# Sparse attention and a gated convolution block on one core: the first head pair turned in float32, mask rows spread by copies, half of the last convolution moved to VectorE, a new written order

## The chip, the cores and the metric

The kernel runs on one core of a Trainium2 chip. The metric is the device time of one execution in microseconds (us); the profiler's span, from the first to the last instruction, is given beside it. The engines are TensorE (PE, with its weight loads shown apart as PEld), VectorE (DVE), ScalarE (ACT), GpSimd (POOL) and SyncE (SP). ACT, POOL and SP also issue DMAs.

## The reference

```python
# attention: q, k, v are (4, 8, 768, 64); blocks of 32 tokens, 24 of them
scores = scale * np.matmul(q, k.transpose(0, 1, 3, 2))
mask = np.abs(blk_i - blk_j) <= 1
mask = mask | (blk_i == 0) | (blk_j == 0) | (blk_i == 23) | (blk_j == 23)
for qb in range(24):
    for kb in sampled_blocks[qb]:            # three drawn blocks per query block
        mask[qb*32:(qb+1)*32, kb*32:(kb+1)*32] = True
attn = softmax(np.where(mask, scores, -1e9))
x = (attn @ v), heads side by side           # (4, 768, 512)
# gated convolution block
h = np.maximum(x @ w_in, 0.0)                # w_in (512, 1024)
conv_out = sum over k of conv_w[k] * h shifted by k - 1 tokens   # three taps
out = (h * sigmoid(conv_out)) @ w_out        # w_out (1024, 512), float32
```

All inputs are float32; the block table is int64.

## The kernel before

**Tiling.** There are 16 head pairs P (four per batch) and eight half-batches of 384 queries; the last half-batch is cut in two parts of 256 and 128 queries, so there are nine segments n. The 768 tokens of a head lie in six groups of 128 by their number modulo a stride, so that a block of 32 tokens is spread over all groups. A unit u is eight blocks of 128 keys by 128 queries: scores (op `s`, line 743, two groups of matmuls that fill one 128x1024 PSUM tile `st`), one exponential on ScalarE (`exp`, line 754, into `pt`), and the product with the values (`av`, line 776). There are 144 units: 18 per half-batch, the ninth segment has 6. With two `st` tiles, scores run at most two units ahead of the exponentials.

**The mask** is part of the matmul: the contraction has 88 rows, 64 of the head and 24 of the mask. The query side of rows 64 to 87 holds -8000 at its own block (`nblk`, line 279, and `m_q`, lines 290 to 303), the key side holds 1 where the block pair is shut, 0 where it may be seen. `a_edges` (line 270) makes the fixed part, `a_rand` (line 282) compares the block numbers with the sampled table `sbi`, and `k_rows` (line 307) writes the 24x384 key rows of the first tile in four strided VectorE instructions (line 313), each of which also turns "may" into "shut". `m_kc` and `m_kh` copy them for the odd key groups and the second head, `m_slot` (line 356) and a DMA (`m_dma`, line 359) for the other four slots of `qk`.

**Loads.** K, Q and V come as float32 from memory. POOL's DMAs cast them to bf16 on the way. The first pair (P = 0, two heads) goes another way: SP and ACT load its float32 data into `o2s` tiles (`first_q`, `first_k`, lines 243 to 256), ScalarE and VectorE cast it to bf16 (`cast_q`, `cast_k`, lines 432 to 441), and TensorE turns it (`k_tr`, line 468, and `q_tr`, line 506) into PSUM, from where copies (`k_cp`, `q_cp`; all plain copies are recorded at lines 327 and 329) bring it to the `qk` tile. SP's first issues are head 0's k, the block table (`ld_sb`, line 254), head 1's q and the convolution weights; ACT's are head 0's q and head 1's k. Pairs 1 to 4 are also turned on TensorE, pairs 5 to 15 by DMA transposes on SP (`xb`, line 583).

**Warm-up.** Until there is something to do, TensorE runs `NWARM` = 45 matmuls on a zeroed tile (`warm`, line 1024), placed among the first transposes.

**After the attention** of a half-batch, each pair's result is normalized (`rcp`, line 692, `norm`, line 694), turned (for a list of places, `X_PE`, on TensorE, line 713, otherwise by DMA on SP, `x_xb`, line 703), multiplied with `w_in` (`f1`, line 892, sixteen groups per half-batch), passed through a relu (lines 912 and 914) into `hE`, convolved, gated and multiplied with `w_out` (`f2`, line 822; the last block at line 807 in two halves). The result is copied out of PSUM (`ev`, into `o2s`) and stored (`out`, line 830).

**The convolution** of two feature groups (a pair, pr = 0 to 3) is six products on VectorE (`mul`, line 946), two sums (`add`, line 956), a tanh on ScalarE (line 995), then `g1` (+1, line 998) and `g2` (times h, line 1003). In the last segment (n = 8, 130 tokens) `CONV_PE = {8: (0, 1, 2, 3)}` puts all four pairs on TensorE instead: six matmuls with diagonal matrices for each (`conv`, line 967), tanh from PSUM (line 972). The 24 diagonals (three for each of eight feature groups) are made by VectorE beforehand (`diag`, line 388).

**Order.** Nothing is scheduled at build time. Every operation is recorded with its dependencies, and the string `ORDER` (line 20) lists the operations in the order in which they are issued, with the engine where there is a choice and the buffer numbers; `put_down` (line 95) walks through it. Each engine then works its own list in that order. The loads on POOL's queue are held back by small copies (`pace`, lines 413 and 657) that wait for a load or an exponential. The costs in the `op(...)` calls served whoever wrote the order; they have no effect when the kernel is built.

Of the kernel before, what the change touches and what calls it, by code (L numbers as in the profile page):

```python
# [7 lines left out]
FP32 = mybir.dt.float32  # L8
# [24 lines left out]
8h02v2u8i8j42Ait17K7L8p18qiZ0i+i/j08r57P7Qiu2rV2j1ivAixiyV8u07U7V7Zj27/02oV2iR28v8w68z17+1858A8B7868aiF18b8f8g
8kiG8E08F8J1iHA2pViSiT808G0iU8K8liI08s08tiJj3iV8L11/18xiKV8R08S8W18y8C8D8H8X20ViW8m121V8T2iL08IiM8Y38/0909142D
2B02E32G2F2Lj51j6j7iX8niO18M941958O2965iNAj88N18U8V9c09d8ZiP8+9293978P2w02x9h19e6iYj9j4iQV9i98jD0993jd39f09j7
ja9ajr19m09n9r19sjejfjgjh8128o8Q9b9o02H12Iis9t1jbjijs9g9k9ljE9w09x9p9q9E19F9u9vjc9y2jFjtjj9G32CV3jk2yV32zV9z
9J09KjujGjHV29O19P9A19L4jvA39T09U0GjM1jJ0jKjLV1jNjOV2M1k522NV4k79Q59V69/1a09Ha409Ia5a17jP0jQjS19B0a61a91aa9M
ab32O2P52R2Q2Z2W2+42X2302/jRVjT9Nae0afk69C9Rj/0k09S9W9Xa20a3ag0k8k9jUAka2JV4k1V9Y1kd0a7aj1akal2jV1ar0asjY0jWkb
9Zkea8acat4aw1axadahaiamjZaB0ay5jXVkfaCan1j+Akg2KVao2apjl1aD6aG1aHaI7auk20k3avaO0k4Akhkl1kmkt3aPazaAaEaFaT1aU
aQ1jx0jmim9D3jw9+2S22T310aq32aV3aY0aZaJaKjnkib11a+0kvknkukc1b2jyb34aL3jojzaR0kokpkjaMkqb60b7be1bfaNjIjpV4jAb85  # L40
kraSaWkB1kwbg6bj0bk3536338bl2391jBV1aXkH0a/b0b4b5bo1b9bpbt0bu2UV0kkkCkIkx2VVkskykzkAbb02YV0bcbq7bv1kJkDkEkKbB1
bCbG0bHkFA033V134V0KkLA3bD3kN1kOkQ0kRkPVbI0bL1bMkSVl92labN4kT1bQ0bRba1kW0kUbV1bS5lclbld3d3a3b3c3e13fjqbhbWbibm
kVAkX3mbd0jCbX6bnbrbsbwc10c2lekYVlh0lic32bxkZ1l30l4bE0c61c7bFby1ljlflkbzl5Acb0cc3j3n03r3oc87k+bJl00bKbObPcd1
37V1lllgl1lmk/Vl2VbTcg1chbUbYco0cpbZ1ci3cq0c4c5c9cacecfct1cub+2lnlp1lqlrl61cjcv4cy0lsczl7b/cA5ckcD1cEcr0cF6cs
cwcxcI0cJcK2l8Vltcl3cBcmlolx3lylzcClL0cQ1luc0bAcnkM3k03p3q3A3B23F3C3D3x3y1lAcRcGcHcLcV0lF1cWcS7lvlBcX3cM1lMlG
lwlClDc+1cTc/d30d00lEd4lHcUlNcYcZd54db1lIdcd1d2dg0lOdhlJA2dd53gV2cN03hVcOlPV4m11m2d6d7m40m5di6lQm3A0m6Adl1dm
dq0md1med82dn2drma0ds1dv1dwmp23lV2mfVmqmbd9m71de0m8cP13s23tkGda3ilK3O3P33E3L3M2dx7msmcVmrm9Amx0mtmzmydD0dEdI1
dF03T3Q3R3S3Z3+3dJmg0dfdjdkdodpdtdN0dudydK4mhdA1dOdS1dTdz1mumiVmF1mHdBmj1mm0mnmkdP3dU5d+0mGd/dGdHe31dLdMdQe4mA
mvmlAmoAe06mIdRdVdWdX3mBe52mJ3uV3mw0mCmD3vVdYlX1lYlZ3w3G03H3U13VdCmKl+e80e9ed1ea1mN3lR0eelSlTlUei0eje10e2dZef7
mEmOmPmQmRlVA1l/A3e6ek0mLmMmSe7eq1mV0ebm/1n0erev0mWewmXes4mT3zV3mUex33IV43WV03XV3NV43/V0n1mYmZA4eA1n2eBeF0eG  # L50
n3A0eC53JVn50n6n81n9eH6n7VnaVnt2eN1eOnk0eP2nlnh1ecninmAnunvnwnxeS0njAeTeU1nyeX1egehelem1nb0eYne1nff00f1etncnJ0
nKeZ7en0eonMngAeueyezf51f6eDeEeIndVf20eJnn1f743Yep2fd0fenoeQ0fi1fjeReVeWe+ff3nznLfk5eK2nB1nCnEnAnDeLnFfn0foe/
f3f4f8fp6fs1ft3KeMm+fa1fu2nq0nrnpVfbf91fgfA0fBfhflfF1fmfGnGnsVnNfC1fqfrfvfwnR3fco31fH7fK0fx3nHfyfLfD0fEfS1fIfT
fJnZ0fM0fznSnTfX0nInOfU4nUnVn+o4fNfYfOg01fV1g1fWnPnQnWfZ3n/o5fP0nXnYg25g80f+o6o0o7A2g9gd1gef/ga60Jo1V40FfQoo1
ol0omopgf2onV1oqAoJ2oKoMgi0gjg3gq1g4o8o2fR3gb0ox0oygrgk1oLg52oNozAoA1gcggoBgs7g6gv0ghgwoCAoD0oEgx0oZ1o+oFAoG1
glgmoHgA1gt1gBoIAgn1or0osgC4p0goo/p50p1p6p7p8g7n4gpm0lWotAgugJ0ou1gygzgKovo90gDoOgO1oaowAp2gL3of1oR3oSp9oPgPob
gEgF3gQ5ocodA2gM0gW0gXoggNoQ1gGgY6gH0ohgRgIAoigS1ps0pth21paoTp3oUgT0oVgUojV4h3h70gZpp1g+oWpuApbh42oXp4pcg/2pJ2
h0gV0h1okoepqh8prApv0pwh91h50h6py1pzpKpB1oYpLpxAhahg1hhpj0hb1pAAhc1hdhi7he1pkplpmhfApMpDpZ0pNpChjhkpnA0pd1pe
hl3hmpOhn0pfpR3pEhoApgpTpSpFpPpUp/qn0qophA3qpApiqk1qlpGqq0qrqD0qmApHpVqEqsApIpWpQqh1qiqy1qzq50q6p+qF1qA2qjAqI0
qJqb1qt1quqcq0q1pXqBq2pYq3qGqv3qdq7q4qeqwqxqK0qN0qHqLqCqOqfV1qMq8qT1qPqQq9V4qaqgpoqRA2qSAqUqVqWqZ0qXV3qYSq+q/  # L60
r0r1Ar2A
# [52 lines left out]
def kernel(  # L114
# [27 lines left out]
    CONV_PE = {8: (0, 1, 2, 3)}  # L142
# [35 lines left out]
    ident24 = sb.tile([NB, NB], FP32, tag="ident24", name="ident24")  # L178
# [7 lines left out]
    may = sb.tile([NB, NB], BF16, tag="may", name="may")  # L186
# [18 lines left out]
    def t_d4(n):  # L205
        return 0.129 + n / 3840.0
# [10 lines left out]
    NWARM = 45  # L217
# [6 lines left out]
    o_amem = op("a_mem", {"DVE": 0.1}, lambda e: nc.vector.memset(A, 1.0), -18, after=[o_warm])  # L224
# [29 lines left out]
    ld_sb = op("ld_sb", {"SP": 0.46}, lambda e: nc.sync.dma_start(out=sbi, in_=sampled_blocks.bitcast(I32)), -21,  # L254
               after=[k0], lat=1.8)
# [804 lines left out]
```

## Time and profile before

| | |
|---|---|
| runs | 208.25, 207.66, 210.04 us; median 208.25 |
| profiled execution | 208.25 us; its span 206.5 us |
| busy in the span | PE 197.2, DVE 184.6, ACT 188.6, POOL 59.3 us |
| granted TensorE clock | 1.00 |
| first exponential begins | 7.46 us |
| last matmuls begin (line 807, 14 of them) | 200.72 us |

In a timeline a line is start, duration, engine, source line, operation and tiles, shapes, and count; brackets hold the idle time of the engine before it and what ended it. An engine name with q (SPq) is the queue that issues DMAs. In a group line, the numbers behind the bar are busy us, the mean ns of one, and idle time before. In a window line, the busy us of PE, PEld, DVE, ACT and POOL follow the window's length. A line of the chain is start, us, and what held the chain.

### The profile page before, as it was taken

How to read it: one execution, taken by the hardware profiler on the slowest of the kernel's cores; microseconds unless marked ns; L12 is line 12 of the kernel's file. 1: busy time of each engine (PE TensorE's matmuls, PEld its weight loads, DVE VectorE, ACT ScalarE, POOL GpSimd, SP SyncE). 2: the span in 40 equal slices, each digit the busy share in tenths (PEclk: the TensorE clock that was granted, in tenths of full speed). 3: DMA queues.
4: the chain of work that ended last, by engine and by line, in shares of the span. 5: the costliest groups of instructions: out<-in, count | busy, mean ns of one | idle time of the engine just before them, and what ended most of it. 6: DMA issues, size and time to landing. Idle time of an engine off the chain costs nothing.

```text
span 206.5 us, 6207 instructions
## 1 busy us (share of the span) xinstructions
PE 197.2 (96%) x2391; PEld 142.9 (69%) x2408; DVE 184.6 (89%) x583; ACT 188.6 (91%) x245; POOL 59.3 (29%) x113
## 2 busy tenths in 40 slices
PE   7899999889999999999999999999999999999992
PEld 7678776766677767766578766765578767686751
DVE  7997779999999988999889986999899979998970
ACT  5899999989999999999899999999899999998731
POOL 8973155351515143401426256400000000000000
PEclk9999999999999999999999999999999999999999
DMA  6999989999497996995958599999101321403106
GB/s 144 174 210 202 182 101 121 183 126 173 81 130 99 128 130 149 168 178 141 99 128 122 71 118 191 150 186 177 20 9 41 92 102 28 166 6 113 51 3 254
DMA packets 51677, 25.54 MB, mean 124 GB/s; under 512 B 37688, under 2 KB 48656, under 8 KB 51648
## 3 DMA queue, kind: packets, MB, share of 16 engines
q0 software_dynamic: 19984, 11.24, 45.7%
q1 hardware_dynamic: 31088, 13.21, 31.9%
q10 hardware_dynamic: 576, 0.69, 0.9%
q8 instruction: 19, 0.31, 0.6%
q14 instruction: 10, 0.08, 0.1%
HBM read 23.08 MB, written 6.29 MB: 142 GB/s over the span
## 4 chain that ended last, share of the span: by engine, by line
PE 72%; DVE 16%; ACT 5%; DMA 3%; issue 2%; SPq 0%; ACTq 0%; DVEq 0%
PE st L743 24%; PE mix L892 16%; PE mix L822 14%; PE av L776 14%; DVE m L946 5%; DVE qk L329 4%; ACT pt L754 3%; DVE m L956 3%; DMA xT<-xtok 2%; DMA sbi<-in_sampled_blocks_dram 1%; DVE xtok L694 1%; PE mix L807 1%; PE st L822 1%; DVE m L998 1%; PE av L967 1%
## 5 line engine op out<-in xcount | busy, mean ns | idle before, releaser
L754 ACT ACTIVATE pt<-st 128x1024 bf16<-128x1024 f32 x144 | 140.4, 1031 | 2.8 <-PE st L743 1.9
L743 PE MATMUL st<-qk 88*128 88x256 bf16 (+2 forms) x600 | 89.1, 267 | 2.4 <-ACT pt L754 1.2
L743 PEld LDWEIGHTS <-qk 88*128 88x128 bf16 x600 | 48.3, 97 | 22.2 <-issue 3.7
L776 PEld LDWEIGHTS <-pt 128*128 128x128 bf16 x1152 | 53.6, 97 | 13.4 <-ACT pt L754 0.7
L776 PE MATMUL av<-vt,pt 128*128 128x65 bf16 x1152 | 59.3, 193 | 0.3
L892 PE MATMUL mix<-xT,winb 128*128 128x384 bf16 (+2 forms) x288 | 53.9, 307 | 0.6 <-ACT o2s L327 0.2
L946 DVE TENSOR_SCALAR m<-hE,cw 128x382 bf16<-128x382 bf16 (+2 forms) x192 | 49.6, 316 | 0.9 <-ACT hE L912 0.7
L822 PE MATMUL mix<-woutb,gT 128*128 128x512 bf16 x159 | 43.8, 379 | 0.6
L956 DVE TENSOR_TENSOR m<-m 128x764 bf16<-128x764 bf16 (+2 forms) x64 | 34.0, 532 | 0.5
L892 PEld LDWEIGHTS <-winb 128*128 128x128 bf16 x288 | 23.9, 97 | 9.5 <-issue 1.3
L995 ACT ACTIVATE m<-m 128x764 bf16<-128x764 bf16 (+2 forms) x32 | 26.1, 824 | 0.6 <-DVE m L956 0.5
L822 PEld LDWEIGHTS <-gT 128*128 128x128 bf16 x184 | 15.8, 97 | 10.0
L415 POOL COPY pace<-pt 1x1 bf16<-1x1 bf16 x24 | 7.8, 323 | 46.6 <-ACT pt L754 45.8
L912 ACT ACTIVATE hE<-mix 128x384 bf16<-128x384 f32 (+2 forms) x37 | 18.2, 496 | 1.1 <-PE mix L892 0.8
L694 DVE TENSOR_TENSOR xtok<-av,rcp 128x384 bf16<-128x384 f32 (+2 forms) x36 | 18.3, 507 | 0.4
L1003 DVE TENSOR_TENSOR gT<-m,hE 128x764 bf16<-128x764 bf16 (+3 forms) x36 | 18.1, 509 | 0.3
L914 DVE TENSOR_SCALAR hE<-mix 128x384 bf16<-128x384 f32 x27 | 14.6, 550 | 3.8 <-PE mix L892 2.7
L239 POOL DMA_DIRECT2D nat<-in_q_dram x23 | 17.0, 741 | 2.0 <-issue 1.8
L329 DVE COPY qk<-mix 64x256 bf16<-64x256 bf16 (+4 forms) x28 | 11.1, 403 | 2.2 <-PE mix L468 1.3
L998 DVE TENSOR_SCALAR m<-m 128x764 bf16<-128x764 bf16 (+3 forms) x36 | 11.9, 337 | 1.0 <-ACT m L995 0.8
L329 DVE COPY qk<-stg 64x1536 bf16<-64x1536 bf16 x22 | 12.0, 549 | 0.2
L239 POOL DMA_DIRECT2D vn<-in_v_dram x16 | 11.5, 716 | 2.2 <-DVE m L956 1.0
(68 smaller groups left out, 113.7 us busy)
## 6 DMA issues: line engine op xcount, KB each, us to landing
out_dram<-o2s SPq DMA_DIRECT2D x22, 256.0 KB, 3.6
vn<-in_v_dram POOLq DMA_DIRECT2D x16, 192.0 KB, 5.4
nat<-in_k_dram POOLq DMA_DIRECT2D x15, 192.0 KB, 4.9
nat<-in_q_dram POOLq DMA_DIRECT2D x7, 192.0 KB, 5.1
winb<-in_moe_w_in_dram POOLq DMA_DIRECT2D x2, 512.0 KB, 9.5
woutb<-in_moe_w_out_dram POOLq DMA_DIRECT2D x4, 256.0 KB, 6.9
nat<-in_q_dram POOLq DMA_DIRECT2D x8, 96.0 KB, 5.5
nq<-in_q_dram POOLq DMA_DIRECT2D x5, 96.0 KB, 5.2
```

Source lines behind the costliest of these rows:

```text
L239: return op(name, {eng: occ}, lambda e: on(e).dma_start(out=dst(), in_=src), prio, deps, dma=(kind, service), **kw)
L329: nc.vector.tensor_copy(out=dst, in_=src)
L694: nm = op("norm", {"DVE": t_dps(128 * C)}, lambda e: nc.vector.tensor_tensor(out=xtok_t[xk.index][:, 0:C].rearrange("p c h d -> p h c d"), ...
L743: nc.tensor.matmul(out=st[:, 128 * x:128 * (x + n_)], lhsT=QK_t[s][0:88, 1, hh, kc, :], rhs=QK_t[s][0:88, 0, hh, at:at + n_, :].rearrange( ...
L754: nc.scalar.activation(out=pt_t[ptb.index], in_=st_t[stb.index], func=AF.Exp, bias=0.0, scale=0.125)
L776: nc.tensor.matmul(out=o[:, off:off + 65], lhsT=pt_t[ptb.index][:, 128 * x:128 * x + 128], rhs=V_t[vslot_b[P].index][:, hh, kc, 0:65], sta ...
L822: nc.tensor.matmul(out=acc(), lhsT=gT_t[gb.index][:, ffc, 128 * t:128 * t + 128], rhs=woutb[:, ffc, :], start=(ffc == 0), stop=(ffc == NFF ...
L892: nc.tensor.matmul(out=mix_t[hb.index][:, w1 * y:w1 * y + w1], lhsT=winb[:, fc, 128 * ffc:128 * ffc + 128], rhs=xT_t[xt_buf[n].index][:, f ...
L912: i = nc.scalar.activation(out=dst, in_=src, func=AF.Relu, bias=0.0, scale=0.5)
L946: i = nc.vector.tensor_scalar(out=m_t[cb.index][:, x, y, 0:w], in0=hE_t[heb.index][:, f0 + y, t0 + x:t0 + x + w], scalar1=cw[:, x, f0 + y: ...
L956: nc.vector.tensor_tensor(out=m[:, a_, :, 0:w], in0=m[:, a_, :, 0:w], in1=m[:, b_, :, 0:w], op=ALU.add)
L995: th = [op("tanh", {"ACT": t_act(2 * w) + 0.04}, lambda e, cb=cb, w=w: nc.scalar.activation(out=m_t[cb.index][:, 0, :, 0:w], in_=m_t[cb.in ...
```

## The change

- *Block table first.* SP's list becomes block table, head 0's q, head 1's q, convolution weights. ACT's becomes head 0's k, head 1's k.
- *Float32 turning.* The casts of the first pair are gone. TensorE turns the float32 data with a float32 identity `identf` (128x128, a VectorE copy of `ident`, where before only a 24x24 one was made), and the copies out of PSUM read float32. The matmuls are three 128x128 for the k of each head, and one of 128 and one of 64 columns for the q of each head. Both heads' turns stand before the first scores in the new order.
- *Mask rows.* The test writes "shut" directly (`not_equal`, `min`), with the fixed part inverted by one more small VectorE operation in `a_edges`. One copy (`m_w`, on ScalarE in the new order) widens 24x24 to 24x384 (`pairs`), and one copy for each of the even and odd key groups spreads it (`m_k`, VectorE). The four strided instructions and `m_kc` are gone.
- *Last convolution.* `CONV_PE = {8: (2, 3)}`: pairs 0 and 1 of the last segment go the VectorE way (12 products, 4 sums), their 12 matmuls and 12 of the diagonals are gone.
- *Warm-up.* `NWARM` = 30; 23 of them stand before the first transposes, where before there were 32.
- *Order.* The whole string is written anew. Where an engine is chosen: relus on ScalarE 39 instead of 37 of 64, evictions on ScalarE 17 instead of 15 of 25, query copies on ScalarE 4 instead of 1 of 22. In the tail two more evictions are on ScalarE.

```diff
-    CONV_PE = {8: (0, 1, 2, 3)}
+    CONV_PE = {8: (2, 3)}
...
-    ident24 = sb.tile([NB, NB], FP32, tag="ident24", name="ident24")
+    identf = sb.tile([128, 128], FP32, tag="identf", name="identf")
+    ident24 = identf[0:NB, 0:NB]
...
-    may = sb.tile([NB, NB], BF16, tag="may", name="may")
+    shut = sb.tile([NB, NB], BF16, tag="shut", name="shut")
+    pairs = sb.tile([NB, S // 2], BF16, tag="pairs", name="pairs")
...
-    NWARM = 45
+    NWARM = 30
...
-    k0 = first_k(0, "SP", -22, [])
-    q0 = first_q(0, "ACT", -22, [])
-    k1 = first_k(1, "ACT", -21, [q0])
-    ld_sb = op("ld_sb", {"SP": 0.46}, ..., -21, after=[k0], lat=1.8)
-    q1 = first_q(1, "SP", -20, [ld_sb])
+    ld_sb = op("ld_sb", {"SP": 0.46}, ..., -22, lat=1.8)
+    k0 = first_k(0, "ACT", -22, [])
+    q0 = first_q(0, "SP", -21.5, [ld_sb])
+    k1 = first_k(1, "ACT", -21, [k0])
+    q1 = first_q(1, "SP", -20, [q0])
...
+        nc.vector.tensor_scalar(out=A[:, 1:NB - 1], in0=A[:, 1:NB - 1], scalar1=-1.0, scalar2=1.0,
+                                op0=ALU.mult, op1=ALU.add)
...
     def k_rows(e):
-        to = E_t[0][64:88, 1, 0].rearrange("j c (a r) -> j c a r", r=16)
-        by = may.rearrange("j (a b) -> j b a", b=3)
...
-        put(to[:, :, :, 0:6], 0)
-        put(to[:, :, :, 10:16], 2)
-        put(to[:, 1:2, :, 5:11], 1)
...
+        dcopy(e, pairs.rearrange("j (b t) -> j b t", t=16), shut.unsqueeze(2).broadcast_to([NB, NB, 16]))
+
+    def k_spread(t):
+        return lambda e: dcopy(e, t[0][64:88, 1, 0], pairs.rearrange("j (p c) -> j c p", c=3))
...
             def fn(e):
+                if P == 0:
+                    for j in range(3):
+                        nc.tensor.transpose(out=bt[mb.index][:, 128 * j:128 * j + 128],
+                                            in_=kf[hs[0]][:, 128 * j:128 * j + 128], identity=identf)
+                    return
                 t = bt[mb.index].bitcast(BF16)
...
-                        w_ = 64 if P == 0 and g == 0 and hh == 0 and y == 1 else 128
+                        w_ = 64 if raw and y == 1 else 128
                         nc.tensor.transpose(out=t[0:w_, 128 * pos:128 * pos + 128], in_=src()[:, c0:c0 + w_],
-                                            identity=ident)
+                                            identity=identf if raw else ident)
```

More of the change, by code (lines that the diff above doesn't have):

```diff
@@ L264 @@
         pattern=[[-1, 128]], channel_multiplier=1), -19, [o_imem])
[L266 to L267 removed]
+    o_i24 = op("ident24", {"DVE": 0.2}, lambda e: nc.vector.tensor_copy(out=identf, in_=ident), -16, [o_ident])
     def a_edges(e):
@@ L432, in kq_transposes @@
         if P == 0:
-            both = {"ACT": 0.42, "DVE": 0.47}
-            cq = [cast("cast_q", lambda x=x: nat_t[nb.index][:, 0, 192 * x:192 * x + 192],
-                       lambda x=x: qf[:, 192 * x:192 * x + 192], -16.5 + 2 * x, [ld_q0[x]], {"ACT": 0.25, "DVE": 0.28},
-                       uses=[nb]) for x in range(2)]
-            ck = [cast("cast_k", lambda x=x: nat_t[nb.index][:, 1, 384 * x:384 * x + 384], lambda x=x: kf[x][:, 0:384],
-                       -16.6 + 2 * x, [ld_k0[x]], both, alloc=[] if x else [nb],
-                       uses=[nb] if x else [])
-                  for x in range(2)]
-            ld_k, ld_q = ck, cq
+            ld_k, ld_q = ld_k0, ld_q0
         else:
```

136 lines of the change are left out of this document (66 added, 70 removed).

## The prediction

> **What bounds the kernel now.** I read the page first (busy shares, chain), then the table of windows, then the timeline of the first 12 us and of the last 20, and last the groups by shape for prices.
>
> ```profile
> PE 197.2 (96%) x2391; PEld 142.9 (69%) x2408; DVE 184.6 (89%) x583; ACT 188.6 (91%) x245; POOL 59.3 (29%) x113
> PE 72%; DVE 16%; ACT 5%; DMA 3%; issue 2%; SPq 0%; ACTq 0%; DVEq 0%
> ...
> 0.00:10.00 10.00, 8.61 (x81) 7.21 (x82) 8.42 (x44) 7.23 (x12) 9.07 (x18) 1.00 0.98 158
> 40.00:50.00 10.00, 8.90 (x127) 6.71 (x125) 9.59 (x27) 9.47 (x12) 4.89 (x11) 1.00 1.16 151
> ...
> 190.00:200.00 10.00, 9.72 (x93) 6.26 (x91) 9.20 (x36) 6.24 (x15) 0.00 (x0) 1.00 0.07 26
> ```
>
> TensorE carries 72% of the chain that ends last, but in the middle VectorE and ScalarE run at 9.59 and 9.47 of 10 us beside it (columns of a window: length, PE, PEld, DVE, ACT, POOL, granted clock, DMA). So no engine has slack there; what can be shortened cleanly is the head, where TensorE does little but warm-up, and the tail, where ScalarE is at 6.24 of 10.
>
> The head, from the timeline:
>
> ```profile
> 0.74 0.40 SPq L239 DMA_DIRECT2D o2s<-in_k_dram  x1
> 1.07 3.59 PE L1024 MATMUL st<-warm 128*128 128x128 bf16 x32 [1.07 <-DVE warm L223]
> 1.20 0.43 SPq L254 DMA_DIRECT2D sbi<-in_sampled_blocks_dram  x1
> 3.61 1.03 ACT L327 CAST nat<-o2s 128x384 bf16<-128x384 f32 x2
> 3.83 0.22 DVE L283 TENSOR_TENSOR hit<-colidx_i,sbi 24x72 f32<-24x72 int32 x1 [0.29 <-DMA sbi<-in_sampled_blocks_dram]
> 4.08 0.30 DVE L285 TENSOR_REDUCE may<-hit 24x24 bf16<-24x96 f32 x1
> 4.61 1.36 DVE L313 TENSOR_SCALAR qk<-may 24x144 bf16<-24x144 bf16 x4
> 5.02 0.47 ACT L327 COPY qk<-mix 64x384 bf16<-64x384 bf16 x1 [0.38 <-PE mix L468]
> 5.58 0.35 ACT L327 CAST nat<-o2s 128x192 bf16<-128x192 f32 x1
> 6.10 0.33 PE L1024 MATMUL st<-warm 128*128 128x128 bf16 x3
> 6.60 0.38 PE L743 MATMUL st<-qk 88*128 88x384 bf16 x2 [0.17 <-DVE qk L329]
> 7.46 3.88 ACT L754 ACTIVATE pt<-st 128x1024 bf16<-128x1024 f32 x4 [0.20 <-PE st L743]
> 10.74 0.29 DVE L329 COPY qk<-mix 64x256 bf16<-64x256 bf16 x1
> 11.50 2.85 ACT L754 ACTIVATE pt<-st 128x1024 bf16<-128x1024 f32 x3 [0.17 <-PE st L743]
> ```
>
> The block table is issued second on SP (1.20), VectorE waits 0.29 us for it, builds the mask rows (four instructions, 1.36 us), and the first scores stand at 6.60 behind a VectorE copy. The first exp runs at 7.46; exps then follow each other at 0.97 us (3.88/4), and the fifth waits again, at 11.50, behind VectorE's copies of the second pair (the last ends at 11.03).
>
> **The change part by part. Block table first.** Issued at 0.74 instead of 1.20, the mask test can start 0.46 earlier, at 3.37, if VectorE is there. Ahead of it VectorE has one more small operation in the edge part and a 128-wide f32 identity where a 24-wide one was; I price the two at up to 0.3 and 0.2 by the 0.22 and 0.30 rows, which the old wait of 0.29 covers in part. So the mask is tested by about 3.9, 0.46 ahead of 4.38.
>
> **Mask rows by copies.** Four instructions (1.36) become one widening copy on ScalarE and one spread per key set on VectorE (0.28 each, the row below), in place of one copy that went before. ScalarE's copy costs 0.47 by the 64x384 row. The price of strided reading is unknown: 0.28 as for contiguous rows, up to 0.34 as the mean of the four (1.36/4). I take 0.3. VectorE is relieved of about 1 us before 8 us.
>
> **Float32 turning, no casts.** Gone: 1.03 + 0.35 on ScalarE and one cast on VectorE. In their place TensorE turns ten 128-wide f32 pieces (six of k, four of q) and the copies read f32. These stand before the first score on TensorE's queue, and three of head 1's copies before the first exp on ScalarE's. The rows for their price:
>
> ```profile
> 4.45 0.53 PE L468 MATMUL mix<-ident,nat 128*128 128x128 bf16 x3
> ...
> L743 PE MATMUL st<-qk 88*128 88x128 bf16 x216 | 40.7, 218 | 0.4 <-ACT pt L754 0.4
> ...
> 15.49 0.17 PE mix L378
> ...
> 3.26 0.28 DVE L329 COPY qk<-qk 24x384 bf16<-24x384 bf16 x1
> 6.89 0.36 DVE L329 COPY qk<-mix 64x384 bf16<-64x384 bf16 x1
> ```
>
> The warm-ups show the array's step in the first 6 us: 32 in 3.59, less 0.31 for the last one's passage, is 0.106 apiece. At 6.10 three take 0.33; with 0.218 for one, that is 0.056. The clock doubles near 6. A bf16 turn costs 0.106 before that (three in 0.53, the last's 0.31 in it). The one f32 turn of the trace (L378, 24 wide) held the chain 0.17 at the doubled clock, so 0.34 at the slow one; if its width counts too, 104 more columns at 0.056 per 128 make 0.22 and 0.43. Ends: 0.106 and 0.43 each; I take 0.34, the nearer kind of row, and 0.17 after 6.0. With 23 warm-ups ahead instead of 32 (end at 1.07 + 23 x 0.106 = 3.5): k of head 0 by 4.6, q by 5.3, k of head 1 by 6.2, q by 6.6, scores of the first unit by 7.1; ScalarE's copies of q, 0.37 + 0.27 (estimates by width from the 0.47 row), end near 7.3. The first exp at 7.3 is 0.15 ahead; at 0.106 each it would come at 6.7, 0.8 ahead; at 0.43 each at 7.8, 0.3 behind. VectorE's list from its k copy to the second pair's q copy took 6.89 to 11.03, 4.1 us, and holds about the same instructions after; begun when k of head 1 is turned and through (6.4), it ends at 10.5. So the fifth exp gains 0.3 to 0.5. I take **-0.4** for the head, between +0.3 and -1.0 (all of it early). From there the stage runs on ScalarE's exps, so the gain carries.
>
> By the Trainium skill, "FP8 and Floating Point Precision", section TensorE Precision Notes, true FP32 takes four passes; four times 0.106 is 0.42 apiece, an estimate, by which the head gains nothing. "TensorE: Matmul & The Clock Gate", Terms, has transpose mode four times faster for FP32, which would be the 0.106 end. No run yet shows which holds.
>
> **Half of the last convolution on VectorE**, and the tail:
>
> ```profile
> L388 DVE TENSOR_SCALAR diag<-ident,cw 128x128 bf16<-128x128 bf16 x24 | 4.6, 249 | 0.1
> L946 DVE TENSOR_SCALAR m<-hE,cw 128x256 bf16<-128x256 bf16 x24 | 5.5, 280 | 0.0
> L956 DVE TENSOR_TENSOR m<-m 128x512 bf16<-128x512 bf16 x8 | 3.4, 419 | 0.1
> ...
> L1003 DVE TENSOR_TENSOR gT<-m,hE 128x260 bf16<-128x260 bf16 x4 | 1.1, 291 | 0.0
> L329 DVE COPY o2s<-mix 128x512 f32<-128x512 f32 x9 | 6.2, 688 | 1.9 <-PE mix L822 1.9
> L327 ACT COPY o2s<-mix 128x512 f32<-128x512 f32 x13 | 7.4, 588 | 2.3 <-PE mix L822 2.0
> ...
> 193.67 0.34 PE av L967 x6
> 190.40 0.29 DVE L694 TENSOR_TENSOR xtok<-av,rcp 128x128 bf16<-128x128 f32 x1
> 199.15 0.28 DVE L1003 TENSOR_TENSOR gT<-m,hE 128x260 bf16<-128x260 bf16 x1
> 200.72 1.69 PE L807 MATMUL mix<-woutb,gT 128*128 128x256 bf16 x14
> 202.45 0.37 ACT L327 COPY o2s<-mix 128x256 f32<-128x256 f32 x1 [0.90 <-PE mix L807]
> ```
>
> TensorE loses 12 of 24 matmuls, two groups of 0.34: -0.68 on the chain. VectorE gains 12 products and 4 sums: at 0.23 (5.5/24, twice as wide, so an upper price) and 0.28, 3.9; at 0.17 and 0.23, as short ones would pack, 3.0. By the order it also enters the tail with three pairs of wide products (0.46 each) and four wide sums (0.42 each) fewer to do after its last normalization, 3.1 less, and one eviction (0.69) before its last gate goes to ScalarE, which has room. Before, its list from that normalization (190.69) to the last gate (199.43) took 8.7; after, 8.7 - 3.1 - 0.7 + 3.0 to 3.9 = 7.9 to 8.8. So the gates come about as early as before, TensorE stays the chain, and it ends (202.4 before, then one eviction) 0.68 sooner. At the worst the first of the new gates, due about 1 us sooner in TensorE's list than a gate was, is 0.9 late: +0.2. I take **-0.5**.
>
> Half the diagonals (12 x 4.6/24 = 2.3) vanish from VectorE between 25 and 185 us; they lie beside TensorE except where VectorE is the chain, 16% of it, so with the two relus that move to ScalarE (which adds 1.0 there) **-0.3**, none at the least and -0.8 at most.
>
> **New order.** Buffers and stages stay; what moves is which projection work stands between the scores. Counted from the two written orders, between the first scores of one half-batch and the next the projection groups differ by at most four. SP's and POOL's queues keep their lists, with neighbours swapped. I take 0. Bounds: TensorE idles 1.1 us in the window at 40, so closing such gaps gives about -1; opening them costs what the third rival says.
>
> **Sum.** The profiled execution took 208.25 us, 206.5 of it span and 1.75 around it; it is also the median of the three runs. 208.25 - 0.4 - 0.5 - 0.3 = **207.05**.
>
> **The rivals.**
>
> One: the best ends meet. Turning is cheap (-1.0), the tail wins its 0.68, VectorE's relief 0.5, the order closes 1.0 of idle: 208.25 - 3.2 = 205.1. For it: every part removes work from a place that the chain passes through. Against it: three engines near 9.5 of 10 take the room of each other.
>
> Two: the head gives nothing, since the change takes away what warms the clock. Before, TensorE works densely from 1.07 until the clock doubles near 6, 4.9 us. After, 23 warm-ups end at 3.5, and turns that wait for loads follow. If the 4.9 us count anew from where turns begin to stand behind loads, about 4.6, the clock doubles at 9.5: all turns cost 0.34 and a unit's eight score blocks 0.85 (8 x 0.106) in place of 0.45: q of head 1 by 7.0, the first scores by 8.1, the first exp at 8.3, 0.8 behind. Units then need 0.85 of TensorE beside 0.97 of ScalarE, so nothing more is lost. 208.25 + 0.8 - 0.8 for the rest = 208.25. The Trainium skill, "TensorE: Matmul & The Clock Gate", Part 1, states a free-running window of about 3.4 us that must be busy, and Part 4 that transposes do not count as busy for it; by that rule this rival holds. The trace of before speaks half against it: it doubled with turns among the warm-ups from 4.45 on.
>
> Three, the slower side: the first projection matmuls of a half-batch now stand sooner after its last attention matmul. By the two orders 18 of TensorE's groups become 13 in between (second half-batch), 38 become 26 (fourth), 35 become 27 (sixth). The sixth already waited:
>
> ```profile
> 135.01 6.69 SPq L583 DMA_TRANSPOSE stg<-nat  x4
> 143.09 4.26 DMA xT<-xtok
> ...
> 148.37 0.44 PE st L743 x4
> ...
> 151.03 0.49 PE av L776 x16
> ...
> 190.16 0.86 PE mix L822 x4
> ```
>
> The first row is SP's queue, the second the chain. Four transposes of keys and queries hold SP for 6.69 us ahead of the token transposes, in both orders, and the 4.26 is on the chain. The sixth loses two score groups (two matmuls each, 0.22), five attention groups (four, 0.12) and one output group (two, 0.43) of cover: 1.5. If SP is no earlier, TensorE stands that much longer there; with a lack of 1.0 at each of the other two, +3.5 in all, of which the savings return 1.2: 210.55. It decides once the stands add up to more than 1.2. Against it: between the token transposes on both sides of these four SP has five issues in the new order instead of seven.
>
> **How the numbers follow.** The forecast case (206.2 to 208.0) 0.38, the best ends 0.24, no gain in the head 0.16, opened waits 0.22 (208.5 to 211.5). One per cent is 2.1 us, about what a measurement can tell from no change: below 206.2 lies the first rival, 0.24; above 210.3 some two thirds of the third, 0.14; 0.62 is within. The predicted time is the forecast case's, 207.0 (207.05 rounded down). The range, 205.1 to 210.1, leaves out about one in ten on each side.
>
> **What would show it.** Right: the mask test at 3.3 to 3.5, the first exp before 7.4, the fifth before 11.3, last matmuls ending before 202 with no wait on the gates. Wrong: f32 turns above 0.4 apiece; the 0.106 step lasting beyond 6.5; a wait of TensorE on the last gates over 0.5; TensorE's idle time between 20 and 190 grown by more than 1 us, above all at the first projections. Any of the last three carries the time past 208.

## The result, and the profile after

The changed kernel takes 206.84 us (median of 20 runs, 206.41 to 208.47), the kernel before 208.26 (20 runs); the ratio is 0.9931, 95% interval 0.991 to 0.9953. Forecast were 207.0, a range of 205.1 to 210.1, and a change within one per cent. Its profiled execution took 206.62, with a span of 204.6; that of before 208.25 and 206.5. A mean granted clock of about 0.992 in the record of an execution stands for one stretch of 3.4 us at half TensorE clock in it (1.7 us lost of some 206), 0.984 for two; ratios leave out executions more than 1.5% above the fastest of their kernel, medians don't.

The page of the changed kernel, busy shares and chain:

```profile
PE 195.2 (95%) x2364; PEld 140.8 (69%) x2381; DVE 182.5 (89%) x578; ACT 189.7 (93%) x249; POOL 58.8 (29%) x113
PE 72%; ACT 14%; DVE 10%; issue 2%
```

TensorE works 2.0 us less (fifteen warm-ups and twelve convolution matmuls are gone) and keeps its 72% of the chain. What VectorE and DMA lose there (16% and 3% before), ScalarE gains (5% before).

The head, from the timeline of the changed kernel (in brackets: idle time before, and what ended it):

```profile
3.17 0.22 DVE L284 TENSOR_TENSOR hit<-colidx_i,sbi 24x72 f32<-24x72 int32 x1 [0.22 <-POOL colidx_i L260]
3.53 0.85 PE L450 MATMUL mix<-identf,o2s 128*128 128x128 f32 x3
4.55 0.46 ACT L319 CAST qk<-mix 64x384 bf16<-64x384 f32 x1
4.82 0.44 PE L502 MATMUL mix<-identf,o2s 128*128 128x128 f32 x2 [0.43 <-DMA o2s<-in_q_dram]
5.04 0.77 DVE L321 CAST qk<-mix 64x384 bf16<-64x384 f32 x2 [0.86 <-ACT qk L319]
5.15 0.50 PE L450 MATMUL av<-identf,o2s 128*128 128x128 f32 x3
5.84 0.36 ACT L319 CAST qk<-mix 64x256 bf16<-64x256 f32 x1 [0.83 <-DVE qk L321]
6.31 0.44 PE L502 MATMUL av<-identf,o2s 128*128 128x128 f32 x2 [0.66 <-DMA o2s<-in_q_dram]
6.69 0.38 PE L740 MATMUL st<-qk 88*128 88x384 bf16 x2
6.88 1.01 ACT L319 CAST qk<-av 64x384 bf16<-64x384 f32 x3 [0.67 <-DVE qk L321]
7.92 5.90 ACT L751 ACTIVATE pt<-st 128x1024 bf16<-128x1024 f32 x6
9.93 1.30 DVE L321 COPY qk<-mix 64x768 bf16<-64x768 bf16 x3
```

The first exp starts at 7.92 instead of 7.46. The turns aren't what delays it: three f32 turns take 0.85, of which the last one's passage is 0.42, so 0.21 apiece at the slow clock; at 5.15 three take 0.50, of which 0.27, so 0.11. The clock has doubled by then. The delay is made on ScalarE: it stands 0.83 us for VectorE's copy out of the bank that it reads next, VectorE stands 0.86 for ScalarE's, then ScalarE 0.67 again. Copies out of one PSUM bank by two engines follow each other in this program; they don't run side by side. And TensorE waits twice for queries. From the first exp on, six follow each other without a pause (5.90), so the fifth, at 11.70, is only 0.20 later than before.

The tail, chain of waits from 182.81 to the end, and the short new products and sums by shape, in the window 182 to 206:

```profile
182.81 0.84 DVE m L943 x4
...
192.78 0.66 DVE m L943 x4
193.44 0.33 DVE gT L1000
193.77 0.35 DVE m L943 x2
194.12 0.04 issue
194.15 1.03 PE mix L819 x4
195.18 0.17 PE av L964 x3
...
199.58 1.76 PE mix L804 x16
201.34 0.02 issue
```
```profile
L943 DVE TENSOR_SCALAR m<-hE,cw 128x130 bf16<-128x130 bf16 x12 | 2.3, 245 | 0.0
L953 DVE TENSOR_TENSOR m<-m 128x260 bf16<-128x260 bf16 x4 | 1.1, 286 | 0.0
```

Each group of diagonal matmuls is 0.17 long on the chain (three) instead of 0.34 (six). VectorE's twelve products cost 0.19 and its four sums 0.28 each. The chain goes over from VectorE to TensorE at 194.15 without a stand: the two are level there, and TensorE ends at 201.34 instead of 202.41.

That is 1.07 of the 1.86 us between the two profiled spans. Nearly all of the rest lies behind the last copy out of PSUM: the execution ends 2.89 us after it, where before it was 3.66. The stores of the output land sooner (last number of a row, us from issue to landing; first before, then changed):

```profile
out_dram<-o2s SPq DMA_DIRECT2D x22, 256.0 KB, 3.6
```
```profile
out_dram<-o2s SPq DMA_DIRECT2D x22, 256.0 KB, 2.3
```

### The profile page after: what moved, and what is told of

It reads as the page before. It is cut to its first block, busy times and chain, and to the rows that moved or that the text cites. A ratio compares the mean times of both kernels' runs of the same rounds, so it can differ in the third digit from the quotient of the medians.

```text
span 204.6 us, 6162 instructions
## 1 busy us (share of the span) xinstructions
PE 195.2 (95%) x2364; PEld 140.8 (69%) x2381; DVE 182.5 (89%) x578; ACT 189.7 (93%) x249; POOL 58.8 (29%) x113
## 4 chain that ended last, share of the span: by engine, by line
PE 72%; ACT 14%; DVE 10%; issue 2%
PE st L740 25%; PE mix L889 16%; PE mix L819 14%; PE av L773 14%; ACT pt L751 9%; DVE m L943 3%; DVE qk L321 2%; DVE m L953 2%; ACT m L992 2%; ACT hE L909 1%; ACT qk L319 1%; PE mix L804 1%; PE st L819 1%; DVE gT L1000 1%; DVE m L995 1%
## 5 line engine op out<-in xcount | busy, mean ns | idle before, releaser
L773 PEld LDWEIGHTS <-pt 128*128 128x128 bf16 x1152 | 51.8, 97 | 12.1 <-ACT pt L751 0.7
L773 PE MATMUL av<-vt,pt 128*128 128x65 bf16 x1152 | 57.5, 193 | 0.2
L889 PE MATMUL mix<-xT,winb 128*128 128x384 bf16 (+2 forms) x288 | 52.3, 308 | 0.1
L943 DVE TENSOR_SCALAR m<-hE,cw 128x382 bf16<-128x382 bf16 (+3 forms) x204 | 51.8, 313 | 0.1
L953 DVE TENSOR_TENSOR m<-m 128x764 bf16<-128x764 bf16 (+3 forms) x68 | 34.7, 516 | 0.3
L992 ACT ACTIVATE m<-m 128x764 bf16<-128x764 bf16 (+3 forms) x34 | 27.2, 803 | 0.6 <-DVE m L953 0.5
L407 POOL COPY pace<-pt 1x1 bf16<-1x1 bf16 x24 | 6.5, 270 | 50.5 <-ACT pt L751 50.4
L909 ACT ACTIVATE hE<-mix 128x384 bf16<-128x384 f32 (+2 forms) x39 | 19.3, 505 | 1.3 <-PE mix L889 1.1
L911 DVE TENSOR_SCALAR hE<-mix 128x384 bf16<-128x384 f32 x25 | 13.8, 550 | 6.7 <-PE mix L889 4.5
L240 POOL DMA_DIRECT2D nat<-in_k_dram x15 | 11.3, 754 | 1.8 <-issue 1.6
```

The costliest lines, as they stand in the source:

```text
L240: return op(name, {eng: occ}, lambda e: on(e).dma_start(out=dst(), in_=src), prio, deps, dma=(kind, service), **kw)
L773: nc.tensor.matmul(out=o[:, off:off + 65], lhsT=pt_t[ptb.index][:, 128 * x:128 * x + 128], rhs=V_t[vslot_b[P].index][:, hh, kc, 0:65], sta ...
L889: nc.tensor.matmul(out=mix_t[hb.index][:, w1 * y:w1 * y + w1], lhsT=winb[:, fc, 128 * ffc:128 * ffc + 128], rhs=xT_t[xt_buf[n].index][:, f ...
L909: i = nc.scalar.activation(out=dst, in_=src, func=AF.Relu, bias=0.0, scale=0.5)
L943: i = nc.vector.tensor_scalar(out=m_t[cb.index][:, x, y, 0:w], in0=hE_t[heb.index][:, f0 + y, t0 + x:t0 + x + w], scalar1=cw[:, x, f0 + y: ...
L953: nc.vector.tensor_tensor(out=m[:, a_, :, 0:w], in0=m[:, a_, :, 0:w], in1=m[:, b_, :, 0:w], op=ALU.add)
```

## The experiments

The kernels e1 to e4 ran on one chip, e5 to e8 on a second, e9 to e11 on a third, e12 on a fourth, each beside runs of the kernel before on the same chip (medians 208.11, 208.18, 208.60, 208.78); the ratio goes by these. Differences of medians between kernels of different chips carry the 0.7 by which these differ.

**e1, the old head with the new rest.** The first loads, casts, bfloat16 turns, strided mask rows and 45 warm-ups of before, up to the first mask copies; from there the new written order, with the new convolution.

```diff
 (source of before, head operations of its ORDER, the rest of the new ORDER)
-    CONV_PE = {8: (0, 1, 2, 3)}
+    CONV_PE = {8: (2, 3)}
```

> The changed kernel with the old head put back (bf16 casts and turns, strided mask rows, loads and warm-ups as before) and everything behind the first exp in the new order, the last convolution half on VectorE. If the head of the change loses time, as the first exps of the two traces say (7.92 against 7.46, still 0.25 late at the 19th), this kernel is 0.25 to 0.45 us faster than the changed one: 206.4 to 206.6, ratio to before 0.991 to 0.992. If the head gained, as the prediction had it (-0.4), it is at 207.2, ratio 0.995. If the head does not matter because the later stages absorb it, 206.8.

Measured: 209.35, ratio 1.0056 (1.0019 to 1.0094), above all three expectations. Without its new head the changed kernel is slower than before. The place is to be seen in the timeline, first of e1, then of the kernel before, and in e1's windows (length, PE, PEld, DVE, ACT, POOL, granted clock, DMA):

```profile
9.10 1.52 DVE L329 COPY qk<-qk 24x1536 bf16<-24x1536 bf16 x2
10.65 1.30 DVE L329 COPY qk<-mix 64x768 bf16<-64x768 bf16 x3
12.00 0.38 PE L743 MATMUL st<-qk 88*128 88x384 bf16 x2 [1.12 <-DVE qk L329]
```
```profile
11.09 0.38 PE L743 MATMUL st<-qk 88*128 88x384 bf16 x2 [0.24 <-DVE qk L329]
```
```profile
10.00:12.50 2.50, 0.92 (x9) 0.48 (x8) 2.36 (x6) 1.45 (x3) 2.43 (x5) 1.00 1.39 188
12.50:15.00 2.50, 2.50 (x37) 2.15 (x36) 1.73 (x5) 1.79 (x2) 2.06 (x4) 0.53 1.31 218
15.00:17.50 2.50, 2.50 (x30) 2.05 (x28) 1.06 (x3) 1.76 (x3) 0.00 (x0) 0.79 1.27 205
```

The new order has VectorE do more copies ahead of the one that the second half of the fifth unit's scores waits for. With the old head's longer list these end at 11.95 (11.23 in the changed kernel, 11.03 before), TensorE works 0.92 of 2.50 us, and behind that its granted clock is 0.53 and 0.79: 0.47 x 2.5 + 0.21 x 2.5 = 1.7 us of its time. In steps of half a microsecond (PE, clock, DMA), the clock is halved from about 12.6 to 16.0, 3.4 us:

```profile
12.00:12.50 0.50, 0.48 (x6) 1.00 1.30 193
12.50:13.00 0.50, 0.50 (x15) 0.64 1.20 172
13.00:13.50 0.50, 0.50 (x8) 0.50 1.54 260
...
15.50:16.00 0.50, 0.50 (x6) 0.50 1.28 202
16.00:16.50 0.50, 0.50 (x11) 0.95 1.36 236
```

All twelve executions of e1 have such a stretch (mean granted clock 0.984 to 0.992). Theory from here: the new order is tight enough that the head's VectorE work decides whether TensorE stands long enough to lose its clock.

**e2, the new head alone**, before the old order and the whole convolution on TensorE.

```diff
 (source of after, head operations of its ORDER, the rest of the old ORDER)
-    CONV_PE = {8: (2, 3)}
+    CONV_PE = {8: (0, 1, 2, 3)}
```

> The kernel before with the new head alone (table first, float32 turns, spread mask rows, 30 warm-ups, new load queues); behind it the old order, the last convolution on TensorE. If the head loses: 208.5 to 208.7, ratio 1.001 to 1.002. If it gains as predicted: 207.85, ratio 0.998. If it is absorbed: 208.25.

Measured: 207.43, ratio 0.9968 (0.9943 to 0.9992). So the head gains, though its first exp comes at 7.91, and from the fifth to the thirty-first exp it is 0.02 to 0.18 behind the profile of before (0.08 ahead from the thirty-second). What it has later, 0.2 near 126 us and 0.5 between 148 and 151, can't be put down to it: e4, with the old head, gains 0.2 and 0.3 on before in the same stretches. A part that may: none of e2's twelve executions has a mean granted clock under 0.99, nine of the 35 of before on that chip have. But without all executions under 0.994 the medians still are 207.43 and 207.88, and where these 0.45 come from isn't shown.

**e3 and e4, the queue of the last store.** The change had also moved one store of the last output from ScalarE's queue to SP's.

```diff
-    out#24 on SP        (changed kernel)
+    out#24 on ACT       (e3; e4 is the reverse, in the kernel before)
```

> The changed kernel with the very last store issued by ScalarE as before instead of SP. In the traces the last copy out of PSUM ends 3.66 us before the end in the kernel before (store on ScalarE) and 2.90 before it in the changed one (store on SP). If the queue makes the difference, this kernel loses 0.75: 207.6, ratio 0.9967. If it is the crowd of stores just ahead of it, which the new order thins out, nothing changes: 206.8, ratio 0.993.

> The kernel before with the very last store on SP instead of ScalarE. If the queue makes the difference: 207.5, ratio 0.9964. If it is the crowd of stores: 208.25, or a few tenths more because SP issues one store after another (0.4 apiece).

Measured: e3 207.15, ratio 0.9955 (0.9917 to 0.9993); e4 208.77, ratio 1.0016 (0.9989 to 1.0044). Neither is told apart from the kernel that it was made of; the store's queue is worth nothing that shows. The profiles agree: from the last copy to the end it is 2.89 in e3 as in the changed kernel, 3.79 in e4 beside 3.66 before. It goes by the written order, not by the queue: 2.87 to 2.89 in nine of the ten profiles with the new order (3.54 in e9), 3.52 to 3.79 in the three with the old. But e3's profiled execution (207.98) shows the changed kernel's head with the clock's doubling late. The same scores there and in the changed kernel's profile:

```profile
10.01 1.06 PE L740 MATMUL st<-qk 88*128 88x256 bf16 x4
11.29 1.92 PE L740 MATMUL st<-qk 88*128 88x384 bf16 x8
```
```profile
8.99 0.60 PE L740 MATMUL st<-qk 88*128 88x256 bf16 x4 [0.20 <-ACT pt L751]
```

Four score matmuls take 1.06 instead of 0.60, the step of the attention matmuls falls from 0.055 to 0.029 us only at 13.5, and the fifth exp starts at 13.31 instead of 11.70. That is the prediction's second rival, in some executions; the four of the changed kernel that took 208.0 to 208.4 at a mean clock of 0.997 to 1.00 would fit it, but none of them was profiled. The column of the granted clock stands at 1.00 throughout: it doesn't show the doubling at the start, only the matmuls' step does.

**e5, the last convolution whole on TensorE again**, all else as changed.

```diff
-    CONV_PE = {8: (2, 3)}
+    CONV_PE = {8: (0, 1, 2, 3)}
```

> The changed kernel with the last convolution whole on TensorE again (24 small matmuls and 24 diagonals instead of 12 and 12; the 12 products and 4 sums leave VectorE's tail). The prediction's step says TensorE's end carries this: 12 matmuls, 0.68, and the diagonals' 0.3 come back, so 207.4 to 207.8. Rival: in the changed kernel VectorE's products and sums carry the chain from 182.8 to 194.1, so taking 3 us of work off VectorE there pays for the 0.68: 206.0 to 206.9.

Measured: 207.97, ratio 0.9998 (0.9967 to 1.0028). Giving the convolution back loses about 1.1 (1.4 by the two ratios, whose intervals don't overlap). In the profiles the sixtieth exp starts 0.38 later than in the changed kernel (VectorE has twelve more diagonals to build, which would fit), the last one 0.40 later, and the span ends 0.88 later (205.5): so 0.4 is lost in the body and 0.5 in the tail. The rival's 206.0 to 206.9 is wrong, and e5's chain shows why:

```profile
PE 86%; ACT 5%; DVE 5%; issue 1%; ACTq 0%
```

With the convolution on TensorE, TensorE alone carries the tail; with half of it moved, the two share it.

**e6, the stand filled.** e1 with 16 matmuls into the part of the score bank that the waiting scores are about to overwrite, ahead of them (the second half of the fifth unit).

```diff
+                for _ in range(fill):
+                    nc.tensor.matmul(out=st[:, 512:640], lhsT=warm, rhs=warm, start=True, stop=True)
```

> The old head with the new rest (e1), and 16 idle matmuls of 128 columns (0.055 each, 0.88 in all) put into the place where TensorE stood 1.12 us for a copy of VectorE at 10.9; the wait itself stays. Theory: the stand itself costs little, but behind it the granted clock was 0.53 from 12.5 to 15 and 0.79 from 15 to 17.5, some 1.7 us of TensorE's time; filled, the clock stays at 1.00 there, the ninth exp starts near 16 instead of 17.86, and the time is 206.9 to 207.6. Rival (the order of the rest simply doesn't fit the old head, whatever the clock): 208.9 to 209.5 as in e1.

Measured: 207.41, ratio 0.9956 (0.9932 to 0.9979). Windows of e6, as for e1 above:

```profile
10.00:12.50 2.50, 1.71 (x21) 1.28 (x20) 2.39 (x5) 1.45 (x3) 2.50 (x6) 1.00 1.34 174
12.50:15.00 2.50, 2.30 (x51) 2.12 (x51) 1.91 (x6) 2.13 (x3) 1.58 (x3) 1.00 1.34 223
```

The scores start at 12.01 as in e1 (12.00), no computation is gained, and the kernel is 1.9 us faster: the ninth exp starts at 16.56 instead of 17.86. The clock was e1's loss. What the old head still costs beside the new one is 207.41 - 206.84 = 0.6, which the intervals don't separate.

**e7, the new mask rows alone in the old head of e1**: a widening copy on ScalarE and two spreads on VectorE instead of four strided writes.

```diff
-        put(to[:, :, :, 0:6], 0)
...
+        dcopy(e, pairs.rearrange("j (b t) -> j b t", t=16), shut.unsqueeze(2).broadcast_to([NB, NB, 16]))
```

> e1 with one part of the new head: the mask rows spread by copies (0.42 each on VectorE, one of 0.51 on ScalarE) in place of four strided writes (1.37 in all); casts, bfloat16 turns and loads stay old. Theory: the strided writes are what makes VectorE late for the third step's copies, so those end 0.4 to 0.6 earlier, TensorE's stand at 10.9 falls from 1.12 to 0.5 to 0.7, and if the clock then holds, 207.0 to 207.7. Rival: the room comes from the float32 turns (no casts) and from the loads, and the stand and the clock's loss remain: 208.8 to 209.5.

Measured: 208.63, ratio 0.9976 (0.9944 to 1.0007), undecided between the two, and the executions say why: five have a mean granted clock of 0.999 or 1.00 and took 206.43 to 207.77, seven have 0.981 to 0.992 and took 208.59 to 210.34. TensorE's stand is 0.87 (expected 0.5 to 0.7). With the clock kept, these five, with old casts and turns, are about as fast as the changed kernel. But the mask rows didn't shorten the stand. VectorE reaches the copies ahead of those scores no earlier than in e1 (9.10), as e7's row shows:

```profile
9.09 1.27 DVE L323 COPY qk<-qk 24x1536 bf16<-24x1536 bf16 x2
```

It was through sooner because these two copies took 1.27 instead of 1.52, and in e9, the same operations, they took 1.52 again. The changed kernel reaches them at 8.60; its head has three copies of queries on ScalarE that e7 has on VectorE, and one of keys the other way round.

**e8, the waits for queries filled with warm-ups** in the changed kernel, three behind the first turned keys, six behind the second.

```diff
-    NWARM = 30
+    NWARM = 39
```

> The changed kernel with nine more warm-up matmuls (0.107 each before the clock doubles), three behind the first pair's first turned keys and six behind the second, where TensorE waited 0.43 and 0.66 us for queries. Theory: in the changed kernel the clock doubles near 5 in one profiled execution and only at 13.0 in another with the same head (e3), where the fifth unit's exp came 1.6 us later; with the waits filled it doubles by about 6.3 each time, so the median falls to 206.4 to 206.8 and the highest time from 208.5 to under 207.6. Rival: the turns themselves, not the waits, leave the window idle for the clock's gate: the times spread as before, median 206.7 to 207.2, highest above 208.

Measured: 206.79, ratio 0.9948 (0.9919 to 0.9977); highest 209.34. The median is as expected, the highest isn't: two executions have a mean granted clock of 0.992. The profile is of one of them (209.34) and shows the loss at another place (rows of TensorE, then windows of TensorE alone, with clock and DMA):

```profile
42.60 0.40 PE L502 MATMUL mix<-ident,nq 128*128 128x128 bf16 x4 [2.32 <-DMA nq<-in_q_dram]
43.90 0.38 PE L740 MATMUL st<-qk 88*128 88x384 bf16 x2 [0.79 <-DVE qk L321]
```
```profile
42.50:45.00 2.50, 1.62 (x25) 0.93 0.86 103
45.00:47.50 2.50, 2.49 (x19) 0.50 1.38 194
47.50:50.00 2.50, 2.29 (x32) 0.89 1.69 131
```

The second queries' transfer is 2.32 us late here, and behind it the clock is halved. The kernel before (e4's profile, 1.09 us of the same wait) has this too. The first doubling came at 7.1 in this profile, not by 6.3. None of the other ten executions took more than 207.41; that the late doubling is gone is not shown by so few.

**e9, e7 with its stand filled** by 13 matmuls as in e6.

> e7 (old casts, bfloat16 turns and loads, new mask rows, new rest) with 13 idle matmuls of 128 columns (0.72 in all) in TensorE's stand of 0.87 at 10.9, so that the clock keeps its 1.00 behind it. Theory: e7's executions in which the clock held took 206.4 to 207.2, as the changed kernel's; with the stand filled all of them do: median 206.5 to 207.1, which says that of the new head only the mask rows are worth anything, and that the float32 turns give time only by keeping the clock. Rival: the clock falls for another reason, median still 208 or more; or the casts cost by themselves, then 207.3 to 207.6 as in e6.

Measured: 207.97, ratio 0.9962 (0.9932 to 0.9993). The stand is covered and the clock holds at 10 to 17.5, but nine executions without a loss took 207.28 to 208.19, not 206.5 to 207.1, and its profile is 0.7 behind the changed kernel from the fifth exp on. So the theory that the mask rows alone are the new head's worth falls. The load queues are worth nothing that shows (e10); the turns without casts and the new shares of ScalarE and VectorE in the copies aren't told apart.

**e10, the old load queues** in the changed kernel.

```diff
-    ld_sb on SP first; k0, k1 on ACT; q0, q1 on SP
+    k0, ld_sb, q1 on SP; q0, k1 on ACT
```

> The changed kernel with the first loads on their old queues (first key tensor, then the block table, then the second query on SP; first query and second key on ScalarE's queue), all else new. Theory: the block table first makes TensorE wait for the queries (0.43 and 0.66 in the changed profile), while the mask test at 3.17 was ended by POOL's column index and not by the table; with the old queues the queries come earlier, the first exp starts at 7.4 to 7.7 instead of 7.92, and the time is 206.3 to 206.8. Rival: the mask rows then come later by the table's 0.3 and the keys hold ScalarE's queue as before: 206.8 to 207.3.

Measured: 207.09, ratio 0.9935 (0.9905 to 0.9965), as the changed kernel. TensorE waits for no query any more, yet the first exp comes later, at 8.21: VectorE now stands for the table, and everything behind it moves. Rows of e10:

```profile
3.82 0.22 DVE L284 TENSOR_TENSOR hit<-colidx_i,sbi 24x72 f32<-24x72 int32 x1 [0.87 <-DMA sbi<-in_sampled_blocks_dram]
7.17 1.01 ACT L319 CAST qk<-av 64x384 bf16<-64x384 f32 x3 [0.67 <-DVE qk L321]
```

The theory (queries set the first exp) falls; the alternation of copies does, and by the thirty-seventh exp (48.06 against 48.05) nothing of it is left.

**e11, work moved into the stand at 40.7** of the changed kernel.

```diff
 PE: ... q_tr#8 av#59
-    s#63 x_tr#4 av#60 av#61
+    x_tr#4 av#60 av#61 s#63
```

> The changed kernel with one token turn (three matmuls) and two attention groups (eight matmuls) taken ahead of the half unit of scores that stood 1.40 us at 40.7 for VectorE's copy of the second queries, nothing else moved. Theory: 0.17 + 0.25 of TensorE's work fits into the stand, so 0.3 to 0.4 is won there and the stand is shorter for the clock: 206.2 to 206.6 (206.84 without). Rival: the exp behind these scores, or the queries' DMA, sets the pace there and nothing is won: 206.7 to 207.0.

Measured: 207.77, ratio 0.9956 (0.9917 to 0.9995), above both expectations. Nothing is won, but for a reason that neither named:

```profile
42.85 0.33 PE L710 MATMUL mix<-ident,xtok 128*128 128x128 bf16 x3 [1.40 <-DVE qk L321]
```

The token turn stands the same 1.40: it writes the PSUM bank that VectorE's copy of the queries has yet to empty. In this profile the clock was lost elsewhere, in the head at 8.1, behind 1.43 us of waiting for head 1's queries.

**e12, that stand filled too**, in e10: 18 matmuls, as in e6, for the second half of unit 31.

> e10 (the changed kernel with the old load queues, whose head doesn't wait for queries) with 18 idle matmuls of 128 columns (0.99 in all) where TensorE stands 1.4 us for VectorE's copy of the second queries, from about 40.7 to 42.1. Theory: this is the second place behind which the clock falls (0.83 between 40 and 50 in the profiles of e4, e7, e8 and e9, some 1.7 us); with both places covered the clock stays at 1.00 in all executions, the window 40 to 50 shows it, median 206.4 to 206.9 and the highest below 207.6: a kernel as fast as the changed one and steadier. Rival: the clock falls there because the queries' transfer is late (2.32 us ahead of their turn in e8), which the filler doesn't cover: some executions stay above 208.4.

Measured: 208.03, ratio 0.9948 (0.9916 to 0.9979). The median misses the 206.4 to 206.9 expected, and three executions stay above 208.4, as the rival had it. In the profile the clock holds between 40 and 45, as expected; it fell in the head instead, where this execution waited for queries and VectorE in pieces of 0.32, 0.66 and 0.19 (windows of TensorE alone):

```profile
5.00:7.50 2.50, 1.52 (x14) 1.00 1.28 169
7.50:10.00 2.50, 2.31 (x18) 0.71 1.36 190
10.00:12.50 2.50, 2.50 (x22) 0.61 1.39 187
```

No kernel tried is told apart from the changed one as faster.

## Why the prediction was right, point by point

- **Head, -0.4.** The way was wrong, and that the size fits is luck. The new head alone is worth -0.7 in the old order (0.9968, 0.9943 to 0.9992) and -2.6 in the new one (1.0056 to 0.9931). But the first exp came 0.46 late where 0.15 early was forecast, and the fifth 0.20 late where 0.3 to 0.5 early was. The step that failed is "ScalarE's copies of q end near 7.3": they had VectorE's copies out of the same banks between them, 0.83 and 0.67 of standing. What e1 and e6 show in its place: in the new order the new head has VectorE through with the copies for the fifth unit at 11.23, not 11.95, and that keeps TensorE's clock. What it gives in the old order, where TensorE stood only 0.24 there, is not located (e2).
- **Mask rows by copies**: 0.3 a spread was taken, the two in the changed kernel took 0.42 each and the widening copy 0.51 instead of 0.47. By e7 and e9 they bring VectorE no earlier to those copies.
- **Price of an f32 turn**, 0.34 and 0.17 taken, between 0.106 and 0.43: measured 0.21 and 0.11, twice a bfloat16 turn's 0.106 and 0.055 (and two of the four pieces of q are 64 wide, not 128). Neither the four passes of the Trainium skill, "FP8 and Floating Point Precision", TensorE Precision Notes, nor a turn as cheap as in bfloat16 (the end that I took from "TensorE: Matmul & The Clock Gate", Terms) agrees with these rows.
- **Block table first**: the test stood at 3.17, 0.2 before the 3.37 named, ended by POOL's index. It is worth nothing that shows (e10).
- **Tail, -0.5, and VectorE's relief, -0.3**: e5 against the changed kernel is -1.1, in the profiles 0.5 in the tail and 0.4 in the body. Both hold in size. VectorE's list in the tail ended at 198.63, 8.2 us after its last normalization, in the 7.9 to 8.8 forecast; the two engines are level, and "TensorE stays the chain" is true from 194.15 on only: from 182.81 the chain runs on VectorE.
- **New order, 0**: e5 against e2 differ in the order alone: 0.9998 (0.9967 to 1.0028) against 0.9968 (0.9943 to 0.9992), not told apart. The zero hides two parts: in these two profiles the last copy ends 0.49 later with the new order (202.62, 202.13), and the time behind it is 0.64 shorter (2.88, 3.52). The third rival's waits, at the first projections of a half-batch, didn't come: DMA is no longer on the chain, where the token transposes had 4.26 us, and the projection matmuls' idle time, in the changed kernel's groups below the last number, is 0.1 us in all. TensorE's idle time between 20 and 190 is 2.8 us in both kernels. What the order does open is the stand at 10.9 with the old head (e1).

```profile
L889 PE MATMUL mix<-xT,winb 128*128 128x384 bf16 (+2 forms) x288 | 52.3, 308 | 0.1
```

- **The second rival** (the clock doubles late) was priced at +0.8 for the head. It happens in some executions (e3's), at 13.5 and not at 9.5, and the fifth exp is then 1.8 later than before: the exps there stand 1.3 to 1.5 apart and wait for scores, where the rival had them follow each other at 0.97. With the same head it happens in one execution and not in another, and this the prediction didn't see.
- The sum, -0.4 - 0.5 - 0.3 = -1.2, against -1.4 measured. That the terms add up was partly luck: -0.7 for the head alone and -1.1 for the convolution alone, with an order that costs between nothing and 0.6; and of the profiles' 1.86, 0.77 lie behind the last copy, where the sum has no term. Of the signs of being right, the mask test came early (3.17), the first and fifth exp late; only the last matmuls, through at 201.34 without a wait on the gates, came as named.

## What to carry to other kernels

When a list on VectorE gets longer ahead of a matmul that waits for it, price the stand not by its own length alone but by what comes after: here 1.1 us of standing cost 1.7 more in clock, and a change that shortens that list can be worth 2.6 us in one order and 0.7 in another. Two changes that pay alone, or don't, have to be tried together and apart before either is priced; here the order without the head was slower than before. Splitting the copies out of one PSUM bank over two engines bought no overlap in this program: each stood for the other.

## What the runs showed of the hardware that I had not expected

- **The clock is lost by the sum of short stands.** It was halved for 3.4 us, a loss of 1.7 each time (e1, e4, e7, e8, e9, e11, e12). In the 3.4 us ahead of the loss TensorE had stood, added up, 1.6 (e1), 1.4 (e7 and e11) and 1.2 (e12), with a longest piece of 1.12, 0.58, 1.43 and 0.66. The Trainium skill, "TensorE: Matmul & The Clock Gate", Why this matters for your kernels, warns of gaps above some 3 us; these runs lose it with much less. The length of the stretch agrees with the 3.4 us of that page's Part 1. Filling the stand with matmuls that compute nothing kept the clock (e6, 1.9 us).
- **The same wait sometimes costs the clock and sometimes doesn't**: a stand of 1.40 near 41 leaves the clock at 1.00 in the changed kernel's profile, first row, and 0.83 in e9's, second.

```profile
40.00:50.00 10.00, 8.18 (x121) 6.13 (x119) 9.27 (x26) 9.72 (x13) 3.21 (x6) 1.00 1.09 149
```
```profile
40.00:50.00 10.00, 8.22 (x111) 6.24 (x109) 8.81 (x26) 8.56 (x11) 3.41 (x8) 0.83 1.43 130
```

  The clock records of the traces show steps of 3.41 us that start at another place in each execution. In e7 two halvings begin at 11.45 and 45.59, ten steps apart; in e11 and e8 the first doubling is at 4.69 and 7.11 and the loss one step and eleven steps later. Counted on from the first doubling in this way, the changed kernel's step with the stand ends at 42.37 and holds 1.40 of standing. In e9 it ends at 44.43 and holds 1.56, because a stand of 0.15 that follows still falls into it; in the changed kernel that one falls into the next step. That agrees with a window that runs free of the program, as the Trainium skill has it in Part 1 of the same page. How much a step bears isn't settled: 1.40 was borne (also in e3 and e5), 1.17 in e12 was not.
- **The first doubling** came at 6.0 before, at 4.8 in the changed kernel, at 13.5 in e3 with the same head, in which TensorE was busy from 1.10 to 5.5 without a pause. Whether the turns didn't count as busy, as the Trainium skill says in Part 4 of that page, is open. The place of the steps alone doesn't explain it: e3's step from 6.63 to 10.05 shows no standing either, and no doubling followed it.
